# Delta rule and MLP on one core: bit masks by wide operations, norms' squares on another engine, a new written order

## The chip, the cores and the metric

The kernel runs on one core of one Trainium2 chip. The metric is the device time of one execution in microseconds, lower is better. A core has TensorE (PE in the profile; PEld is its weight load), VectorE (DVE), ScalarE (ACT), GpSimd (POOL) and SyncE (SP, which only issues DMAs here).

## The reference

```python
# q, k, v: (4, 8, 768, 48), beta: (4, 8, 768)
k_n = k / (np.linalg.norm(k, axis=-1, keepdims=True) + 1e-06)
for t in range(768):
    y[:, :, t] = q_t @ state
    v_old = state^T k_t
    state = state + beta_t * outer(k_t, v_t - v_old)
x = y as (4, 768, 384)              # 8 heads of 48 side by side
xn = (x - mean) / sqrt(var + 1e-06) * g_ln
out = x + relu(xn @ w_ch1) @ w_ch2  # 384 -> 1536 -> 384
```

All values are float32, but the two weight matrices arrive as 64-bit floats, which the kernel converts to float32 itself.

## The kernel before

The 768 tokens are cut into 12 chunks of 64 (`C`). Within a chunk the recurrence is a triangular system: with G the products of the chunk's keys, scaled by beta and the norms, the kernel needs the inverse of a unit triangular 64x64 matrix for each of 32 heads. These stand as 16 blocks on each half of the 128 partitions, in two halves `g` of 8.

Chunk 0 gets its inverse by doubling (`first_inverse`): from 1x1 blocks to 2x2 and so on to 64x64. Each of the steps n = 1 to 5 is a product E (`prod_e`, L720), a `copy_predicated` by mask n on DVE that keeps only the elements that this step adds (L727), a product Z (`prod_z`, L737), a transpose on DVE (`nat`, L685) and three copies on ACT (`back`, L679). It begins with mask 0 on the scaled products (L693, L702, L708). Both halves g go through it side by side. The chunks after it get their blocks of 32 rows on DVE, a column at a time (`rows_inverse`, L827 to L863, two instructions a column), while PE does other work, and the 32-blocks are joined on PE (`join`).

The masks: bit n of (row XOR column) has to be the highest that is set, and bit n of the row (for n = 0, of the column) must be set. The set-up writes `xor` and `bits` with two iotas on POOL, and makes each of the six masks with three DVE instructions on 128x64 integers (L395, L402, L408), in scratch that lies in `xb`, the tile in which `rows_inverse` works later: its memset (L827) has to wait for the masks. `eye`, the identity, is copied into six tiles (`BEGIN`), in which the doubling's steps accumulate (L421 on POOL, L426 on ACT).

`first_norms` makes for chunk 0 the norms of k: ACT squares (L594), DVE sums (L595), ACT takes the root (L596), DVE adds 1e-6 (L597), multiplies the result by itself (L598), takes the reciprocal (L599) and multiplies by beta (L602). A square root of `eps` (L439) runs early on ACT, so that the table of the root is loaded by then.

`recur` does a chunk: the u product (L996), y, the new state, the layer norm; `mlp(0)` runs as plain products in two halves, later chunks by schemes with fewer products (seven instead of eight, fifteen instead of eighteen). The weights come in pieces (`fetch`, on ACT's DMA queue) into `words` and `h_all` and are converted by two ACT instructions (L524, L532), one on DVE (L529) and an addition on POOL (L542).

Nothing is issued in program order. Each step is added to a list with what it reads and writes, and `ORDER`, a string of step numbers written out in the file, says in which order all are issued (`z` is a warm-up product on zeros). `in_this_order` then holds each engine's queue, and the queue of DMAs over SP and ACT, to this order. So each engine works strictly down its own list, and an instruction that waits holds up all behind it on that engine. The numbers `0.17`, `port=2` and so on beside a step are the planner's costs and do nothing at run time.

Of the kernel before, what the change touches and what calls it, by code (L numbers as in the profile page):

```python
# [9 lines left out]
I32 = mybir.dt.int32  # L10
# [6 lines left out]
C = 64  # L17
# [46 lines left out]
146 232 230 149 326 150 219 669 154 z 209 234 155 156 208 231 233 210 158 157 251 46 235 164 160 162 327 200 161 328 239 201 411 159 413 165 170 166  # L64
# [136 lines left out]
def kernel(  # L201
# [150 lines left out]
    def c_pool(fn, cost, w, r=(), pr=-200, **kw):  # L352
        add("Pool", cost, fn, r, w, pr=pr, **kw)
# [1295 lines left out]
```

## Time and profile before

| | |
|---|---|
| three timed runs | 507.06, 510.91, 511.09 us (median 510.91) |
| the profiled execution | 506.83 us, its span 505.1 us |
| PE | 485.9 us busy (96%), 9606 matmuls |
| PEld | 445.7 us busy (88%) |
| DVE | 355.2 us busy (70%), 774 instructions |
| POOL | 275.7 us busy (55%) |
| ACT | 249.0 us busy (49%) |
| DMA | 54.99 MB, of 196097 packets 186076 under 512 B |
| TensorE's granted clock, mean | 0.973; 0.5 from about 14.7 to 21.2, 25 to 32 and 42 to 55.7 us |

Busy time is the time in which an engine has an instruction in work, as a share of the span of 505.1 us. The span is the profiled execution from its first to its last instruction; the execution's own time is 1.7 us longer. The mean of an engine over the whole span hides that the first 50 us are limited otherwise than the rest, so the profile is read by stage.

### The profile page before, as it was taken

To read this page: it belongs to the slowest core of one execution; us is meant where nothing else is said; L and a number is where in the kernel's file an instruction comes from. 1 tells how busy PE (TensorE), PEld (TensorE's weight loads), DVE (VectorE), ACT (ScalarE), POOL (GpSimd) and SP (SyncE) were. 2 spreads that over 40 slices of the span, in tenths; PEclk is the share of its full clock that TensorE was granted. 3 is DMA by queue.
4 is the path that set the end of the run, shared out by engine and by line. 5 is a ranking of instruction groups with operands and counts; after the bars stand their busy time and mean duration, and the time that the engine had idled before them with its cause. 6 is when DMAs were issued, how large, how long until landed. Compare 5 with 4: busy or idle time off the path is not lost.

```text
span 505.1 us, 22184 instructions
## 1 busy us (share of the span) xinstructions
PE 485.9 (96%) x9606; PEld 445.7 (88%) x9606; DVE 355.2 (70%) x774; ACT 249.0 (49%) x620; POOL 275.7 (55%) x430
## 2 busy tenths in 40 slices
PE   6777999999999999999999999999999999999996
PEld 3666988688988898899999999999999999999996
DVE  9689987997699458886559898478899238143251
ACT  5777772633645434636444544436563347363230
POOL 5464527255754595629893462591642851645643
PEclk9776799999999999999999999999999999999999
DMA  8979896756646676448734434765245412111101
GB/s 173 308 153 187 270 189 79 107 138 133 90 87 106 192 127 114 46 100 205 155 41 64 102 55 153 150 91 87 57 85 136 82 23 58 43 50 46 31 12 31
DMA packets 196097, 54.99 MB, mean 109 GB/s; under 512 B 186076, under 2 KB 189404, under 8 KB 196000
## 3 DMA queue, kind: packets, MB, share of 16 engines
q1 hardware_dynamic: 189920, 40.58, 42.1%
q10 hardware_dynamic: 3872, 9.83, 6.1%
q0 software_dynamic: 2208, 3.17, 3.7%
q8 instruction: 75, 1.23, 1.0%
q14 instruction: 22, 0.18, 0.1%
HBM read 36.64 MB, written 16.91 MB: 106 GB/s over the span
## 4 chain that ended last, share of the span: by engine, by line
PE 78%; DVE 13%; SPq 3%; issue 2%; POOL 1%; DMA 1%; ACT 1%; ACTq 0%; DVEq 0%; POOLq 0%
PE f L1419 31%; PE f L1217 22%; PE f L1296 6%; DVE xb L863 4%; DVE tmp L856 4%; SPq L349 3%; PE by L1020 2%; PE two L1013 2%; PE by L979 2%; PE by L771 2%; PE two L979 2%; PE two L1030 1%; PE two L771 1%; PE by L894 1%; PE by L900 1%
## 5 line engine op out<-in xcount | busy, mean ns | idle before, releaser
L1406 POOL TENSOR_TENSOR h_all<-h_all 128x256 f32<-128x256 f32 x123 | 90.2, 746 | 133.3 <-PE f L1419 103.7
L1419 PE MATMUL f<-w_sb,h_all 128*128 128x192 f32 x492 | 109.5, 332 | 0.0
L1419 PE MATMUL f<-words,h_all 128*128 128x192 f32 x396 | 84.5, 330 | 0.3 <-POOL h_all L1406 0.3
L1419 PEld LDWEIGHTS f<-w_sb,h_all 128*128 128x128 f32 x492 | 81.8, 190 | 1.8 <-DVE o L1437 0.2
L863 DVE TENSOR_TENSOR xb<-xb,tmp 128x87 f32<-128x87 f32 (+21 forms) x186 | 73.7, 396 | 4.8
L856 DVE TENSOR_TENSOR tmp<-xb,gb 128x87 f32<-128x87 f32 (+21 forms) x186 | 73.1, 393 | 4.9
L1237 DVE TENSOR_TENSOR h_all<-h_all,f 128x512 f32<-128x512 f32 x96 | 63.6, 682 | 14.2 <-PE f L1217 13.1
L1419 PEld LDWEIGHTS f<-words,h_all 128*128 128x128 f32 x396 | 66.6, 190 | 1.7 <-POOL h_all L1406 1.0
L1296 PE MATMUL f<-xnt,w_sb 128*128 128x256 f32 x216 | 50.2, 382 | 0.0
L349 POOL DMA_DIRECT2D tb<-in_k_dram x64 | 41.9, 660 | 10.3 <-DVE kt L751 9.4
L1239 ACT ACTIVATE h_all<-h_all 128x512 f32<-128x512 f32 x48 | 28.5, 624 | 34.4 <-DVE h_all L1237 34.0
L1296 PEld LDWEIGHTS f<-xnt,w_sb 128*128 128x128 f32 x216 | 40.2, 190 | 5.2
L1233 ACT COPY h_all<-f 128x512 f32<-128x512 f32 x48 | 26.3, 590 | 33.9 <-PE f L1217 17.1
L1437 DVE TENSOR_TENSOR o<-f,x 128x192 f32<-128x192 f32 x33 | 11.6, 352 | 41.8 <-PE f L1419 25.9
L1217 PE MATMUL f<-words,w_sb 128*128 128x128 f32 x256 | 31.7, 276 | 0.0
L1305 ACT ACTIVATE h_all<-f 128x256 f32<-128x256 f32 x36 | 13.4, 383 | 34.8 <-PE f L1296 34.8
L1217 PEld LDWEIGHTS f<-words,w_sb 128*128 128x128 f32 x256 | 30.0, 192 | 0.2
L1217 PE MATMUL f<-xnt,w_sb 128*128 128x128 f32 x192 | 25.4, 276 | 0.0
L542 POOL TENSOR_TENSOR w_sb<-words 128x768 uint32<-128x768 uint32 (+1 forms) x11 | 15.0, 1364 | 17.7 <-DVE words L529 16.7
L1217 PEld LDWEIGHTS f<-xnt,w_sb 128*128 128x128 f32 x192 | 23.7, 192 | 0.1
L1322 PEld LDWEIGHTS f<-xnt,w_sb 128*128 128x128 f32 x144 | 19.5, 203 | 3.4 <-ACT h_all L1330 0.2
L1084 ACT ACTIVATE xnt<-xnt,g_sb 128x256 f32<-128x256 f32 x27 | 12.5, 499 | 19.2 <-DMA xnt<-xld 19.1
(246 smaller groups left out, 955.0 us busy)
## 6 DMA issues: line engine op xcount, KB each, us to landing
words<-in_moe_w_ch_dram ACTq DMA_DIRECT2D x10, 768.0 KB, 7.8
gd<-gsb SPq DMA_DIRECT2D x11, 512.0 KB, 3.9
v<-in_v_dram SPq DMA_DIRECT2D x24, 192.0 KB, 4.2
kr<-in_k_dram SPq DMA_DIRECT2D x46, 96.0 KB, 3.9
out_dram<-o SPq DMA_DIRECT2D x44, 96.0 KB, 2.4
xld<-xlt SPq DMA_DIRECT2D x9, 384.0 KB, 3.0
xnt<-xld SPq DMA_DIRECT2D x36, 96.0 KB, 3.3
gb<-gd SPq DMA_DIRECT2D x44, 64.0 KB, 3.0
```

Of the source, the lines that this page charges most:

```text
L349: add(eng, cost, lambda: QUEUE[eng].dma_start(out=out_, in_=in_), r, w, bulk=n * ns / 16e3, **kw)
L856: lambda j=j, n=n, w=w, t=t: nc.vector.tensor_tensor(out=t, in0=xv[:, 0:n, j : j + 1].to_broadcast([np_, n, w]), in1=gv[:, j : j + 1, j + ...
L863: "DVE", dve(n * w), lambda t=t, rest=rest: nc.vector.tensor_tensor(out=rest, in0=rest, in1=t, op=ALU.subtract),
L979: nc.tensor.matmul(dst[half(e), hp, j], src[drows(hp), (e if n else key_half(c, hp, e)) * GP + j], s_all[drows(hp), e, j], start=(n == 0 o ...
L1217: nc.tensor.matmul(wide(p[:, 128 * n : 128 * n + 128]), w[n // 2][:, n % 2 * 128 : n % 2 * 128 + 128], r, start=start and n == 0, stop=Tru ...
L1233: add("ACT", act(512), lambda: nc.scalar.copy(o, p), pk, ok)
L1237: add("DVE", dve(512), lambda: nc.vector.tensor_tensor(out=o, in0=o, in1=p, op=op), pk, ok)
L1239: add("ACT", act(512), lambda: nc.scalar.activation(o, o, ACTF.Relu), [], ok)
L1296: nc.tensor.matmul(p[:, 0:TOK], w1_sb[:, t, f * 128 : (f + 1) * 128], xnt[:, t], start=(t == 0), stop=(t == KC - 1))
L1322: nc.tensor.matmul(p[:, 0:128], w1_sb[:, t, f * 128 : (f + 1) * 128], xnt[:, t, cols], start=(t == 0), stop=(t == KC - 1))
L1406: add(eng, cost, lambda: e.tensor_tensor(out=out_, in0=x, in1=y, op=op), r, w, port=2 if eng == "Pool" else 1, pr=-2)
L1419: lambda f=f, t=start and f == 0: nc.tensor.matmul(p[:, 0:D2], lhs(f), rhs[:, f], start=t, stop=(f == F2 - 1), skip_group_check=True),
```

## The change

The six masks are made at once. POOL writes a third iota (`steps`, the numbers 0 to 5). `both` holds the row (or column) number shifted left by 16 and joined with `xor`; one shift of it by all values of `steps` (a 128x5x64 operation for masks 1 to 5, a 128x64 one for mask 0), one AND with 65536 + 63 and one comparison with 65537 give the masks: a field of the low bits that is 1 after the shift and a set bit 16. In `first_norms` the DVE product is replaced by a Square on ACT with `eps` as bias, on the root before 1e-6 is added. `ORDER` is written anew for all 2981 steps (2991 before); every other step does what it did.

```diff
     c_pool(lambda: nc.gpsimd.iota(bits, pattern=[[1, C]], base=0, channel_multiplier=0), 0.2, ["bits"])
+    flat = xb.rearrange("p s t -> p (s t)").bitcast(I32)
+    rows_, both, steps = flat[:, 960:1024], flat[:, 832:960].rearrange("p (n t) -> p n t", t=C), flat[:, 800:806]
+    wide = flat[:, 0 : 6 * C].rearrange("p (n t) -> p n t", t=C)
+    c_pool(lambda: nc.gpsimd.iota(steps, pattern=[[1, 6]], base=0, channel_multiplier=0), 0.15, ["steps"])
...
     MASKED = (0, 1, 2, 3, 4, 5)
-    for n in MASKED:
...
-            lambda t1=t1, k_=k_, w=w: nc.vector.tensor_scalar(
-                out=t1, in0=xor[:, 0:w], scalar1=w - 1, scalar2=k_, op0=ALU.bitwise_and, op1=ALU.logical_shift_right
...
-            lambda t2=t2, k_=k_, own=own: nc.vector.tensor_scalar(
-                out=t2, in0=own, scalar1=k_, scalar2=1, op0=ALU.logical_shift_right, op1=ALU.bitwise_and
...
-            lambda m=m, t1=t1, t2=t2: nc.vector.scalar_tensor_tensor(
-                out=m, in0=t1, scalar=1, in1=t2, op0=ALU.is_equal, op1=ALU.mult
...
+    for n, (own, key) in enumerate(((bits, "bits"), (rows_, "rows"))):
+            lambda n=n, own=own: nc.vector.scalar_tensor_tensor(
+                out=both[:, n], in0=own, scalar=16, in1=xor, op0=ALU.logical_shift_left, op1=ALU.bitwise_or
...
+    for n in range(2):
+        ns_ = slice(0, 1) if n == 0 else slice(1, 6)
...
+            lambda n=n, ns_=ns_, m_=m_: nc.vector.tensor_tensor(
+                out=wide[:, ns_], in0=both[:, n : n + 1].to_broadcast([128, m_, C]),
+                in1=steps[:, ns_, None].to_broadcast([128, m_, C]), op=ALU.logical_shift_right,
...
+            lambda ns_=ns_: nc.vector.tensor_scalar(
+                out=wide[:, ns_], in0=wide[:, ns_], scalar1=65536 + C - 1, scalar2=None, op0=ALU.bitwise_and
...
+            lambda ns_=ns_: nc.vector.tensor_scalar(
+                out=small[:, ns_].bitcast(I32), in0=wide[:, ns_], scalar1=65537, scalar2=None, op0=ALU.is_equal
...
             add("ACT", 0.21, lambda ss=ss, nr=nr: nc.scalar.sqrt(nr, ss), ks, kn_, **kw)
+            add("ACT", 0.21, lambda nr=nr, nd=nd: nc.scalar.activation(nd, nr, ACTF.Square, bias=eps), kn_ + ["eps"], kd, **kw)
             add("DVE", 0.17, lambda nr=nr: nc.vector.tensor_scalar_add(nr, nr, 1e-6), [], kn_, port=2, **kw)
-            add("DVE", 0.17, lambda nr=nr, nd=nd: nc.vector.tensor_tensor(out=nd, in0=nr, in1=nr, op=ALU.mult), kn_, kd, port=1, **kw)
             add("DVE", 0.2, lambda nd=nd: nc.vector.reciprocal(nd, nd), [], kd, port=2, **kw)
```

The new file is seven lines longer, so a line number of the changed kernel from L428 on is that of the kernel before plus 7 (L529 is L536 there).

At the head of the queues the new order is this. SP issues one of the four pieces of chunk 1's k before its two pieces of chunk 0's k. ACT issues the first 768 KB weight piece right behind its two pieces of chunk 0's k; then come two copies of `eye`, the root of `eps`, a third copy, and then the squares. POOL writes the three iotas and issues both beta rows, and copies `eye` twice before the second instruction of PE's identity `ident`; from the L834 memset of `xb` (which waits for masks 1 to 5) on, conversions, the scaling of v and DMA issues follow. DVE makes masks 1 to 5 up to the comparison, then `eye`, then mask 0; the comparison for masks 1 to 5 stands behind the first transposes of the doubling. From about 50 us on, PE's list is that of before with neighbouring steps exchanged.

More of the change, by code (lines that the diff above doesn't have):

```diff
@@ L59 @@
 ORDER = """
[4 rows of a table removed]
-146 232 230 149 326 150 219 669 154 z 209 234 155 156 208 231 233 210 158 157 251 46 235 164 160 162 327 200 161 328 239 201 411 159 413 165 170 166
[88 rows of a table removed]
+6 37 4 42 45 8 9 53 40 39 58 11 52 12 41 3 0 10 5 15 44 19 61 20 46 14 1 13 16 17 26 22 43 24 18 62 27 55 38 7 28 50 234 318 25 34 67 78 71 64 68 66
+63 72 69 79 23 65 85 73 70 51 74 80 86 81 75 217 76 54 77 83 87 60 82 100 88 z 89 84 106 90 101 59 194 91 207 102 103 92 107 205 112 105 108 195 110
[91 rows of a table added]
 """
@@ L375 @@
     c_pool(lambda: nc.gpsimd.iota(bits, pattern=[[1, C]], base=0, channel_multiplier=0), 0.2, ["bits"])
+    flat = xb.rearrange("p s t -> p (s t)").bitcast(I32)
+    rows_, both, steps = flat[:, 960:1024], flat[:, 832:960].rearrange("p (n t) -> p n t", t=C), flat[:, 800:806]
+    wide = flat[:, 0 : 6 * C].rearrange("p (n t) -> p n t", t=C)
+    c_pool(lambda: nc.gpsimd.iota(steps, pattern=[[1, 6]], base=0, channel_multiplier=0), 0.15, ["steps"])
     c_dve(
-        lambda: nc.vector.tensor_scalar(out=xor, in0=xor, scalar1=C - 1, scalar2=None, op0=ALU.bitwise_and),
-        0.17, ["xor"], port=2,
+        lambda: nc.vector.tensor_scalar(out=rows_, in0=xor, scalar1=C - 1, scalar2=None, op0=ALU.bitwise_and),
+        0.17, ["rows"], ["xor"], port=2,
     )
     c_dve(
-        lambda: nc.vector.tensor_tensor(out=xor, in0=xor, in1=bits, op=ALU.bitwise_xor), 0.22, ["xor"], ["bits"], port=1,
+        lambda: nc.vector.tensor_tensor(out=xor, in0=rows_, in1=bits, op=ALU.bitwise_xor), 0.22, ["xor"], ["rows", "bits"], port=1,
     )
-    flat = xb.rearrange("p s t -> p (s t)").bitcast(I32)
     c_dve(
@@ L386 @@
     )
-    c_dve(
-        lambda: nc.vector.tensor_tensor(out=flat[:, 960:1024], in0=xor, in1=bits, op=ALU.bitwise_xor), 0.22, ["rows"], ["xor", "bits"], port=1,
-    )
     MASKED = (0, 1, 2, 3, 4, 5)
-    for n in MASKED:
-        k_, m, w = n, masks[n], C
-        t1, t2 = (flat[:, C * i : C * i + w] for i in (2 * n, 2 * n + 1))
+    for n, (own, key) in enumerate(((bits, "bits"), (rows_, "rows"))):
         c_dve(
-            lambda t1=t1, k_=k_, w=w: nc.vector.tensor_scalar(
-                out=t1, in0=xor[:, 0:w], scalar1=w - 1, scalar2=k_, op0=ALU.bitwise_and, op1=ALU.logical_shift_right
+            lambda n=n, own=own: nc.vector.scalar_tensor_tensor(
+                out=both[:, n], in0=own, scalar=16, in1=xor, op0=ALU.logical_shift_left, op1=ALU.bitwise_or
@@ L397 @@
             ),
-            0.17, [("ma", n)], ["xor"], port=2,
+            0.22, [("both", n)], [key, "xor"], port=1,
         )
-        own = flat[:, 960 : 960 + w] if n else bits[:, 0:w]
+    for n in range(2):
+        ns_ = slice(0, 1) if n == 0 else slice(1, 6)
+        m_ = ns_.stop - ns_.start
         c_dve(
-            lambda t2=t2, k_=k_, own=own: nc.vector.tensor_scalar(
-                out=t2, in0=own, scalar1=k_, scalar2=1, op0=ALU.logical_shift_right, op1=ALU.bitwise_and
+            lambda n=n, ns_=ns_, m_=m_: nc.vector.tensor_tensor(
+                out=wide[:, ns_], in0=both[:, n : n + 1].to_broadcast([128, m_, C]),
+                in1=steps[:, ns_, None].to_broadcast([128, m_, C]), op=ALU.logical_shift_right,
@@ L404 @@
             ),
-            0.18, [("mb", n)], ["bits", "rows"], port=2,
+            0.08 + 0.07 * m_, [("ma", n)], [("both", n), "steps"], port=1,
         )
         c_dve(
-            lambda m=m, t1=t1, t2=t2: nc.vector.scalar_tensor_tensor(
-                out=m, in0=t1, scalar=1, in1=t2, op0=ALU.is_equal, op1=ALU.mult
+            lambda ns_=ns_: nc.vector.tensor_scalar(
+                out=wide[:, ns_], in0=wide[:, ns_], scalar1=65536 + C - 1, scalar2=None, op0=ALU.bitwise_and
             ),
-            0.22, [("mask", n)], [("ma", n), ("mb", n)], port=1,
+            0.1 + 0.04 * m_, [("ma", n)], [], port=2,
@@ L412 @@
         )
-    MASK_SCRATCH = [(x, n) for x in ("ma", "mb") for n in MASKED] + ["rows"]
+        c_dve(
+            lambda ns_=ns_: nc.vector.tensor_scalar(
+                out=small[:, ns_].bitcast(I32), in0=wide[:, ns_], scalar1=65537, scalar2=None, op0=ALU.is_equal
+            ),
+            0.1 + 0.04 * m_, [("mask", k) for k in range(ns_.start, ns_.stop)], [("ma", n)], port=2,
+        )
+    MASK_SCRATCH = [("ma", 0), ("ma", 1), ("both", 0), ("both", 1), "rows", "steps"]
     BEGIN = [(kts[2], "kt", 2), (gsbs[2], "g", 2), (gsbs[3], "g", 3), (xts[2], "xt", 2), (xts[3], "xt", 3), (pts[1], "pt", 1)]
```

183 rows, old and new, of the table ORDER are left out of this document.

## The prediction

> **What bounds the kernel now.** I read the page's head, the busy table by stage, TensorE's waits, and then the timeline of the first 26 us. By stage:
>
> ```profile
> core 0: us, PE busy (x) PEld busy (x) DVE busy (x) ACT busy (x) POOL busy (x), PEclk, DMA share, GB/s
> 0.00:6.00 6.00, 3.41 (x5) 1.24 (x6) 4.98 (x13) 1.55 (x3) 4.96 (x15) 1.00 0.60 103
> 6.00:12.00 6.00, 4.83 (x90) 3.20 (x90) 5.82 (x28) 4.63 (x12) 1.65 (x3) 1.00 1.13 242
> ...
> 40.00:50.00 10.00, 7.69 (x224) 6.87 (x228) 8.76 (x30) 7.85 (x20) 5.13 (x6) 0.60 0.93 166
> ...
> 100.00:300.00 200.00, 199.32 (x4277) 182.69 (x4276) 152.39 (x321) 93.30 (x244) 126.57 (x197) 1.00 0.58 111
> 300.00:490.00 190.00, 190.00 (x3286) 184.17 (x3285) 115.05 (x235) 90.77 (x211) 92.86 (x155) 1.00 0.34 73
> ```
>
> From 50 us to 490 us PE stands idle 0.7 us in all: there the order of PE's queue costs nothing and PE's own work (the same in both programs) sets the time. Before 50 us PE is idle for 14 us, and VectorE (DVE) is the fullest engine (5.82 of 6 us, 8.76 of 10): this is chunk 0's doubling inverse, a chain of matmuls E1, Z1 ... E5, Z5 with a masked copy and transposes on DVE between them. What shortens this chain brings PE's full stretch forward by as much, and the end with it. Why DVE is late there:
>
> ```profile
> 1.90 1.47 DVE L395 TENSOR_SCALAR xb<-u 128x64 int32<-128x64 int32 x1
> ...
> 2.26 1.28 ACT L439 ACT_TABLE_LOAD   x1 [2.26 <-issue]
> ...
> 3.80 2.38 DVE L402 TENSOR_SCALAR xb<-xb 128x64 int32<-128x64 int32 x1
> ...
> 5.93 0.52 ACT L594 ACTIVATE xln<-kr 128x384 f32<-128x384 f32 x1 [2.18 <-DMA kr<-in_k_dram]
> ...
> 8.10 0.54 DVE L595 TENSOR_REDUCE ksum<-xln 128x8 f32<-128x384 f32 x1
> ...
> 13.47 0.69 PE L720 MATMUL two<-qt,gsb 64*64 64x64 f32 x32 [0.19 <-DVE qt L708]
> ...
> 19.99 1.13 PE L737 MATMUL by<-xt,gsb 64*64 64x64 f32 x32
> ...
> 22.60 1.38 DVE L529 TENSOR_SCALAR words<-words 128x384 uint32<-128x384 uint32 x1
> ...
> 24.58 0.39 PE L771 MATMUL f<-qt,kt 48*64 48x64 f32 x10 [2.41 <-issue]
> ```
>
> Each row: start, length, engine, line, operation, and in brackets the idle time before it and what ended it. A mask step (L395, L402) takes 0.2 us alone (3.59 and 3.70 in the same timeline), but 1.47 and 2.38 us while GpSimd (POOL) runs memsets or copies; the L529 step, 0.33 us alone, took 1.38 us beside POOL's L542. The first half's squares (L594) end at 6.45 us, and their sum (L595) starts only at 8.10, behind masks. E1 starts at 13.47, the second half's Z1 at 19.99, and E2 behind it at 20.8. At 22.17 PE stops for 2.41 us for no cause that the profile shows.
>
> **The change, part by part.**
>
> *Masks.* DVE loses 22 narrow set-up steps and gets 11 (777 instructions become 764 with the two norm steps). Before, DVE was busy 4.98 and 5.82 us of the first two 6 us. The wide steps are not in the trace. The 128x320 shift lies between L863 at 64x240 (0.40) and L693 at 128x512 (0.68): 0.5, nearer the first. The 128x320 TENSOR_SCALAR steps lie between 0.33 (L529, 128x384, alone) and 1.38 (beside POOL): 0.35 each, because POOL stands waiting both times: first for `eye`, then, in its L834 memset of xb, for the wide mask itself. POOL's new iota stands behind two beta DMA issues (0.72 and 0.53), done at about 2.95; the wide shift waits for that. Shift, and, one 64-wide step and a memset follow, so `eye` comes at about 4.35 (3.40 before). ident's affine_select, now behind two POOL copies of `eye` (0.6 each), ends at about 5.9 (3.70 before). Chunk 0's k, landing at 5.93 before, covers that; without this cover each us that `eye` is late would be a us of PE's first transposes.
>
> *ScalarE (ACT).* Two norm products (0.16 each) leave DVE, two Squares (0.2, like L596's square root) join ACT. But the copies of `eye` now stand ahead of the square root that warms the table, and the built program holds two table loads for the one before: 1.28 us more. ACT: two k DMAs and the weight DMA to 2.6, load to 3.9, `eye` at 4.35, two copies (0.52 apart) to 5.4, load to 6.7, root and copy to 7.4. The squares start at 7.4 instead of 5.93. SP now issues a piece of chunk 1's k first (0.64 us), and the 768 KB weight DMA goes at 2.2 instead of 7.04 us, beside k: chunk 0's k lands at 6.5 to 7.2, inside ACT's delay.
>
> The Trainium skill ("ScalarE: Activation LUTs", What ACT_TABLE_LOAD costs) puts a switch of sets at 1.28 us and a drain of 1.38 us behind it. The trace shows 1.28 and the next activation 0.01 us later (2.26 + 1.28, then 3.55), so I add no drain; by the page the gain summed below would shrink by 1.38 us, to almost nothing.
>
> *To E2.* Squares to 8.3; two kt copies and the first root to 9.55 on ACT, the second kt copy to 10.1, the first Square at 10.25, the second at 10.65. On DVE 0.17 + 0.20 + 0.17 + 0.20 + 0.1 follow: the first gsb product starts at about 11.2 (11.15 before). Now both halves are multiplied first (0.65 + 0.1 + 0.63), then the masked copy (0.73) and transpose (0.72): E1 at 14.05, **0.6 later**. The second half: E1 at 14.05 + 1.45 = 15.5 (16.94 before). Wide mask 0.35, masked copies 0.73 + 0.27 + 0.73 to 17.55. Its Z1 then waits only for four q transposes, not eight: about 18.0 (19.99). E2 at about 18.65 against 20.8: **2.1 us earlier**.
>
> *E2 to the first u product (L996).* PE's 2.41 us stop lies 350 matmuls into its queue; I keep it at that count. Z2 then ends at 23.2 (25.74), E3 starts at 26.2 (29.3). Between E3 and E5 stand five weight steps L536 (0.33 to 1.38 each), and POOL, held until the wide mask, now works through copies, conversions and DMA issues without a pause from 16 to 32 us. beta_f's second DMA, at 22.20 before, goes at about 27.8 and took up to 6.1 to land: it holds DVE's db_b step until 33 or so, with a masked copy of E4 behind it. E5 comes at 37.6 with cheap steps and at 40.2 with dear ones (40.10 before), so 2.5 earlier to 0.1 later; the middle is 1.2 earlier. From E5 to the u product before: 45.92 - 40.10 = 5.8, of which 0.48 is a stop. After: DVE does four small steps, a weight step, a query product (0.62), a transpose and then the masked copy, 0.6 to 1.2 us later than before; the q/k transposes and Z5 that follow wait for less. I give 0.4 us of gain: **1.6 us earlier** in all. Bounds: 6.0 earlier (3.1 at E3 kept, 0.5 of the second stop, 2.4 of the first gone) and 5.6 later (below).
>
> *The rest.* Step by step PE's order after 50 us is the old one with neighbours exchanged (mean shift under 0.2 us of PE work in every stretch of 60 steps), and PE has the same 4839 instructions. The last 14 products of the tail come in nearly the same order. Cost: nothing, hidden by PE's full queue; without it each shift would count once.
>
> Sum: profiled execution 506.83 (span 505.1 and 1.7 around it) - 1.6 = 505.2. The four executions shown, 506.83, 507.06, 510.91 and 511.09, have the mean 508.97; the profiled one lies 2.1 below it and 4.1 below the median. TensorE's clock was 0.5 in three stretches between 14.7 and 55.7 us and full elsewhere; where these fall I can't forecast. I predict from the mean: 508.97 - 1.6 = **507.4**.
>
> **The rivals.**
>
> *A larger gain.* DVE sheds its masks, E and Z of both halves alternate without holes, and the 2.41 us stop vanishes as its traffic moves. 3.1 + 0.5 + 2.4 = 6.0: 503.0. For it: PE has 14 us of holes to give, the second half's Z1 waited for work that has moved. Against: the stop sits at a place in the queue that both have.
>
> *Slower: POOL and DVE collide.* Place: 16 to 38 us. POOL's queue stands behind the wide mask, then runs solid; each L536 on DVE waits for a POOL conversion. Seven of them (two of chunk words, five to E5) at 1.38 instead of 0.33 are 7.3 us; beta_f's late landing adds 1. Less the lead of 2.1 and 0.6 that it covers: 5.6 later, 514.6. It decides from a mean L536 of 0.7 us on, where the lead is gone. For it: the 2.38 and 1.38 rows. Against: L529 at 31.15 and 35.88 took 0.34 each with POOL at work, so not every one is caught.
>
> *The lead is eaten.* E2 comes earlier, but the weight steps or the k DMAs take all of it before the first u product: 509.0. For it: two table loads and the dearer E5 stage. Against: 2.1 us at E2 by rows.
>
> **How the numbers follow.** Forecast 0.45 (range 504 to 509.5 alone), larger gain 0.30, eaten 0.12, slower 0.13. A difference of 1% (5.1 us) is about what a measurement here can tell. The first and third cases are within it (0.57), the second beyond it (0.30), the fourth beyond it (0.13). The range takes in the gain's 503.0 less half the runs' spread (2.1) and stops short of most of the slower case: 501.0 to 513.5.
>
> **What would show it.** Right: two table loads on ACT, squares at about 7.4, E1 near 14, E2 near 18.7, the u product near 44, then PE full with the same 455 us of work. Wrong: E2 later than 20.8 (the head's delays counted too low), L536 above 0.7 on average, PE holes after 50 us (the new order is not neutral), or no stop on PE near matmul 350 (then the larger gain).

## The result, and the profile after

The changed kernel takes 511.10 us (median of 21 runs, 509.03 to 513.81), the kernel before 509.38 us (21 runs, 506.47 to 511.89). The ratio is 1.0046 (95% interval 1.0028 to 1.0064): 2.3 us slower, where 1.6 us faster was forecast; within 1%, but on the other side. The profiled execution of after has a span of 508.5 us, that of before 505.1; the one of before was a quick one (506.83 against a median of 509.38), so the 3.4 us between the two profiles are more than the runs show. The mean granted clock is 0.977 (0.973 before) and explains none of it.

By stage (busy time and number of instructions of PE, PEld, DVE, ACT, POOL, then the granted clock, the DMA share and GB/s), kernel after:

```profile
core 0: us, PE busy (x) PEld busy (x) DVE busy (x) ACT busy (x) POOL busy (x), PEclk, DMA share, GB/s
...
6.00:12.00 6.00, 2.42 (x17) 1.78 (x17) 0.62 (x3) 2.34 (x5) 1.24 (x3) 1.00 1.28 196
...
50.00:60.00 10.00, 7.74 (x199) 6.91 (x191) 8.87 (x18) 5.77 (x18) 5.37 (x5) 0.58 0.81 232
...
100.00:300.00 200.00, 199.80 (x4209) 181.59 (x4207) 150.48 (x322) 93.27 (x249) 123.64 (x191) 1.00 0.59 114
300.00:490.00 190.00, 190.00 (x3405) 183.94 (x3405) 116.17 (x240) 89.10 (x211) 92.65 (x155) 1.00 0.35 74
```

From 60 us on PE is idle for 0.5 us in all up to 490 us (0.7 before): it is full, as before. The loss lies in two stretches. From 6 to 12 us PE is busy 2.42 us (4.83 before) and DVE 0.62 (5.82 before): everybody waits, while the DMA engines are full. From 50 to 60 us a second hole has opened. The timeline of after says why:

```profile
2.26 0.65 ACTq L349 DMA_DIRECT2D words<-in_moe_w_ch_dram  x1
...
2.92 0.49 DVE L402 TENSOR_TENSOR xb<-xb 128x320 int32<-128x320 int32 x1 [0.37 <-POOL xb L379]
2.94 1.28 ACT L433 ACT_TABLE_LOAD   x1 [2.94 <-issue]
...
4.10 0.13 DVE L388 TENSOR_SCALAR u<-u 128x64 f32<-128x64 int32 x1
...
5.41 1.28 ACT L446 ACT_TABLE_LOAD   x1
...
9.87 0.94 ACT L601 ACTIVATE xln<-kr 128x384 f32<-128x384 f32 x2 [2.45 <-DMA kr<-in_k_dram]
9.89 1.09 PE L575 MATMUL by<-ident,kr 128*128 128x128 f32 x4 [3.58 <-DMA kr<-in_k_dram]
...
12.39 0.58 ACT L580 COPY kt<-by 128x512 f32<-128x512 f32 x1 [1.59 <-PE by L575]
...
17.90 0.69 PE L727 MATMUL two<-qt,gsb 64*64 64x64 f32 x32
...
22.53 0.69 PE L727 MATMUL two<-qt,gsb 64*64 64x64 f32 x32
...
39.16 0.18 DVE L847 TENSOR_TENSOR db_b<-db_b,beta_f 64x32 f32<-64x32 f32 x1 [0.58 <-DMA beta_f<-in_beta_dram]
...
52.80 1.90 DVE L956 TENSOR_SCALAR xln<-x,mv 128x384 f32<-128x384 f32 x1
...
52.99 1.48 POOL L549 TENSOR_TENSOR w_sb<-words 128x768 uint32<-128x768 uint32 x1
...
54.75 0.90 PE L1099 MATMUL two<-ident,xln 128*128 128x128 f32 x3 [2.26 <-DVE xln L956]
```

The kernel before, at the places that match:

```profile
20.89 0.94 PE L720 MATMUL two<-qt,gsb 64*64 64x64 f32 x32
...
45.92 0.98 PE L996 MATMUL two<-v,xt 64*64 64x48 f32 x25 [0.48 <-issue]
...
49.95 0.40 DVE L949 TENSOR_SCALAR xln<-x,mv 128x384 f32<-128x384 f32 x1
...
51.18 0.90 PE L1092 MATMUL two<-ident,xln 128*128 128x128 f32 x3
```

Chunk 0's k lands at 9.87 us (5.93 before). E1 starts at 17.90 (13.47 before), E2 at 22.53 (20.89 before). At 52.80 the layer norm's step, 0.40 us before, takes 1.90 beside POOL's addition, and PE waits 2.26 us for it.

### The profile page after: what moved, and what is told of

The parts are those of the page before. It is cut to its first block, busy times and chain, and to the rows that moved or that the text cites. A ratio compares the mean times of both kernels' runs of the same rounds, so it can differ in the third digit from the quotient of the medians.

```text
span 508.5 us, 22143 instructions
## 1 busy us (share of the span) xinstructions
PE 486.5 (96%) x9606; PEld 444.8 (87%) x9606; DVE 349.0 (69%) x761; ACT 248.0 (49%) x623; POOL 276.7 (54%) x431
## 3 DMA queue, kind: packets, MB, share of 16 engines
q8 instruction: 75, 1.23, 1.0%
## 4 chain that ended last, share of the span: by engine, by line
PE 89%; DMA 3%; ACT 2%; POOL 1%; DVE 1%; issue 1%; SPq 1%; ACTq 0%; DVEq 0%; POOLq 0%
PE f L1426 31%; PE f L1224 22%; PE f L1303 10%; PE f L1329 3%; PE f L1344 3%; PE by L1027 2%; PE by L986 2%; PE two L986 2%; PE two L1020 2%; PE by L778 2%; PE two L778 2%; PE two L1037 2%; DMA kr<-in_k_dram 1%; DMA beta_f<-in_beta_dram 1%; PE by L901 1%
## 5 line engine op out<-in xcount | busy, mean ns | idle before, releaser
L1426 PE MATMUL f<-w_sb,h_all 128*128 128x192 f32 x492 | 108.2, 331 | 0.0
L1303 PE MATMUL f<-xnt,w_sb 128*128 128x256 f32 x216 | 51.8, 385 | 0.1
L1303 PEld LDWEIGHTS f<-xnt,w_sb 128*128 128x128 f32 x216 | 39.8, 190 | 6.5 <-ACT xnt L1114 0.8
L1224 PE MATMUL f<-words,w_sb 128*128 128x128 f32 x256 | 33.1, 278 | 0.0
L1065 ACT ACTIVATE x<-by 128x384 f32<-128x384 f32 x23 | 11.1, 489 | 26.8 <-PE by L1027 18.4
L1224 PEld LDWEIGHTS f<-xnt,w_sb 128*128 128x128 f32 x192 | 23.6, 192 | 0.1
L629 POOL TENSOR_TENSOR v<-v,knrm 128x768 f32<-128x768 f32 x11 | 16.7, 1520 | 12.3 <-DMA v<-in_v_dram 11.9
```

What stands on the lines that cost most here:

```text
L1224: nc.tensor.matmul(wide(p[:, 128 * n : 128 * n + 128]), w[n // 2][:, n % 2 * 128 : n % 2 * 128 + 128], r, start=start and n == 0, stop=Tru ...
L1303: nc.tensor.matmul(p[:, 0:TOK], w1_sb[:, t, f * 128 : (f + 1) * 128], xnt[:, t], start=(t == 0), stop=(t == KC - 1))
L1426: lambda f=f, t=start and f == 0: nc.tensor.matmul(p[:, 0:D2], lhs(f), rhs[:, f], start=t, stop=(f == F2 - 1), skip_group_check=True),
```

## The experiments

Most are the changed kernel with steps moved in `ORDER`; e6 is the kernel before with one step moved, and m1, m2, m2b and h2 mix the two. Ratios are to the kernel before on the same chip, with the 95% interval (0.001 is 0.5 us); they, not the medians, are compared between runs of different chips. The changed kernel's is 1.0046. Two runs whose ratios lie less than about 1.3 us apart are not resolved by their intervals.

### What makes k late

```diff
 ACT: k of chunk 0 (2 pieces)
-     first weight piece, 768 KB          (e1, e3)
 ...  squares, first kt copy
+     first weight piece, 768 KB          (e1, e3)
-SP:  one piece of chunk 1's k            (e2, e3)
 SP:  k of chunk 0 (2 pieces)
+     one piece of chunk 1's k            (e2, e3)
```

> The changed kernel with one step moved: the first 768 KB weight transfer is issued on ScalarE behind the first kt copy, where the kernel before has it, and no longer at 2.26 us right behind chunk 0's k. Theory W (the weight transfer shares the DMA engines with the small packets of k and holds them up): chunk 0's k lands at 6.0 to 7.0 us instead of 9.87; the squares then wait for ScalarE's second table load and start at about 7.4; E1 of the first half at about 15.4 instead of 17.9, E2 about 20.3 instead of 22.5; the time 1.5 to 2.5 us below the changed kernel's. Theory S (the piece of chunk 1's k that SP issues ahead of chunk 0's pieces is what delays them): k still lands after 9.2 us, E1 after 17.2, the time within 0.5 us of the changed kernel's.

> The changed kernel with one step moved: SP issues its two pieces of chunk 0's k first, and the piece of chunk 1's k behind them. Theory S: k lands at 6.0 to 7.0 us, squares at about 7.4, E1 at about 15.4, the time 1.5 to 2.5 us below the changed kernel's. Theory W: k lands only the 0.6 us of one issue earlier (9.2 to 9.9), E1 at 17.2 to 17.9, the time within 0.7 us of the changed kernel's.

> The changed kernel with both moves: the weight transfer behind the first kt copy, and chunk 0's k first on SP. Both theories: k lands at 5.9 to 6.5 us as before. Then the second table load on ScalarE (5.41 to 6.69) is what the squares wait for: they start at about 7.4, 1.5 us later than in the kernel before; E1 15.0 to 15.6, E2 19.6 to 20.4. If a loss at the start passes through to the end, the time is 2.0 to 2.8 us below the changed kernel's, so about level with the kernel before (within 0.6 us). If the later losses (beta_f's transfer, the layer norm's step that stood 1.9 us beside GpSimd) are losses of their own and not of the late k, less than 1 us comes back.

The transplant, in the kernel before:

```diff
 ACT: k of chunk 0 (2 pieces)
+     first weight piece, 768 KB
 ...  first kt copy
-     first weight piece, 768 KB
```

> The kernel before with one step moved: the first 768 KB weight transfer is issued on ScalarE right behind its two pieces of chunk 0's k, as the changed kernel does, and everything else stays. Theory W: chunk 0's k lands at 8.5 to 10 us instead of 5.93, E1 at 16 to 17.5 instead of 13.47, and the time is 2 to 3.5 us above the kernel before, as far as nothing behind it absorbs the delay. Theory S: k lands at 5.9 to 6.5 us, E1 at 13.5 to 14.1, the time within 0.6 us of the kernel before.

Timeline of the run with the weights later, and then of the kernel before with the weights early:

```profile
6.46 0.63 PE L575 MATMUL by<-ident,kr 128*128 128x128 f32 x4 [0.15 <-DMA kr<-in_k_dram]
...
7.33 0.93 ACT L601 ACTIVATE xln<-kr 128x384 f32<-128x384 f32 x2
...
7.94 0.37 ACTq L349 DMA_DIRECT2D words<-in_moe_w_ch_dram  x1
```

```profile
2.25 0.64 ACTq L349 DMA_DIRECT2D words<-in_moe_w_ch_dram  x1
...
9.54 0.52 ACT L594 ACTIVATE xln<-kr 128x384 f32<-128x384 f32 x1 [5.12 <-DMA kr<-in_k_dram]
```

Theory W holds both ways: taking the weight transfer away brings k from 9.87 to 6.46, adding it to the kernel before takes k from 5.93 to 9.54, and there it costs 2.7 us (512.23 us, ratio 1.0054, 1.0026 to 1.0081). The order on SP alone moves k to 9.37 only (e2: 511.87 us, 1.0048, 1.0028 to 1.0069). The Trainium skill ("DMA: Bandwidth & Descriptors", Queues, rings and completion order) says that each DMA engine takes turns between the queues it has work for, a packet at a time; these landings agree with that, since k's pieces on SP's queue land later when weights are issued on ACT's; the turns themselves no run here shows.

But the end hardly came back: e1 511.04 us (1.0034, 1.0011 to 1.0056), e3 510.37 us (1.0023, 1.0000 to 1.0046), against an expected 1.5 to 2.8 us less than the changed kernel; 0.6 and 1.1 us less were measured, neither resolved. E1 came at 15.7 in e1 and only at 16.4 in e3. The timeline of e3 shows the next obstacle on ACT:

```profile
13.98 0.55 ACT L531 ACTIVATE words<-words 128x384 f32<-128x384 f32 x1 [3.52 <-DMA words<-in_moe_w_ch_dram]
...
14.43 1.05 ACT L580 COPY kt<-f 128x512 f32<-128x512 f32 x2
```

The new order put the first weight conversion ahead of chunk 1's kt copies, which suits early weights. With later weights it waits 3.52 us for them, and the copies and E1 behind it.

### The conversions behind the copies

```diff
 ACT: (as e3)
-     three conversions of the first weight piece
      kt copies of chunk 1, first xt copies
+     three conversions of the first weight piece
```

> The run with both moves at the start (weight transfer behind the first kt copy, chunk 0's k first on SP), and besides ScalarE's three conversions of the first weight piece put behind the first copies of chunk 1's kt and of xt, as the kernel before has them; in that run the first conversion waited 3.52 us for the weights, and the kt copies and E1 behind it. Theory Q (the queue of ScalarE was what kept the early k from paying): the kt copies of chunk 1 at about 11.5 us, E1 at 13.6 to 14.0 instead of 16.4, E2 at 18.3 to 19.0; if that holds to the end, 2.5 to 3 us less than that run, so 1.5 to 2.5 us below the kernel before. Rival P (further on the order has places that are tied to other work, the weight steps on VectorE at 27 to 30 us and E3 of the second half at 32.1 us in both runs): E2 early as said, but E3 of the second half still after 31.5 us, and the time within 0.8 us of that run.

Measured 509.37 us (1.0015, 0.9995 to 1.0036), 1.6 us below the changed kernel. E1 started at 13.66 as theory Q said; E2 only at 20.51, and E3 of the second half at 30.55, between the two theories. The time, 0.4 us below e3, is what rival P said. Its timeline, PE and DVE:

```profile
17.30 0.37 PE L727 MATMUL by<-qt,gsb 64*64 64x64 f32 x2 [1.58 <-issue]
...
26.22 0.52 DVE L536 TENSOR_SCALAR words<-words 128x768 uint32<-128x768 uint32 x1
27.72 0.56 DVE L536 TENSOR_SCALAR words<-words 128x768 uint32<-128x768 uint32 x1 [0.98 <-ACT words L531]
...
27.97 0.45 PE L727 MATMUL two<-qt,gsb 64*64 64x64 f32 x13 [1.05 <-issue]
...
28.20 0.44 DVE L692 STREAM_TRANSPOSE qt<-by 128x256 f32<-128x256 f32 x1
...
30.55 1.13 PE L727 MATMUL by<-qt,gsb 64*64 64x64 f32 x32 [2.13 <-ACT xt L686]
...
40.69 0.58 PE L744 MATMUL by<-xt,xt 64*64 64x64 f32 x11 [2.19 <-issue]
```

Two things hold it: two weight steps on DVE (one waits for ACT) ahead of the transposes of the second half, and stops of PE for which the profile names no releaser ("issue").

### The layer norm's step

```diff
 DVE: column step, column step
+     layer norm of chunk 0 (L956)
      weight step (L536)
      column step (L863)
-     layer norm of chunk 0 (L956)
```

> The changed kernel with one step moved: the layer norm's step of chunk 0 (L956) stands on VectorE ahead of a weight step (L536 at 52.04 us) and a column step (L863 at 52.51), so that it runs at about 52.1 us while GpSimd issues DMAs, and not at 52.8 beside GpSimd's L549 (52.7 to 54.2). Theory C (the collision is a loss of its own, on the path to TensorE's full stretch): L956 takes 0.4 to 0.6 us instead of 1.90, TensorE's wait ahead of L1099 falls from 2.26 us to 0.2 to 0.7, and the time falls by 1.5 to 2.0 us. Rival (that wait is slack of the order, and TensorE then waits as long for the next steps): the wait moves to L1003 or L1329, the time stays within 0.5 us of the changed kernel's.

```profile
51.71 2.13 POOL L349 DMA_DIRECT2D tb<-in_k_dram  x2
...
52.70 0.41 DVE L956 TENSOR_SCALAR xln<-x,mv 128x384 f32<-128x384 f32 x1
...
53.39 0.90 PE L1099 MATMUL two<-ident,xln 128*128 128x128 f32 x3
...
53.85 1.48 POOL L549 TENSOR_TENSOR w_sb<-words 128x768 uint32<-128x768 uint32 x1
```

Theory C holds: beside POOL's DMA issues the step takes 0.41 us, PE's 2.26 us wait is gone, and the time is 509.65 us (1.0019, 1.0006 to 1.0032), 1.4 us below the changed kernel. The move does two things: the step is 1.5 us shorter, and two steps of 0.9 us together no longer stand ahead of it; the run doesn't part them. The Trainium skill ("SBUF — State Buffer", Who interferes with whom) says that some VectorE operations, `tensor_scalar` among them, can use a port pair that they share with GpSimd, and that the loser waits for the other's whole instruction. 1.90 us beside a 1.48 us addition and 0.41 away from it agree with that; which of the two was issued first the rows leave open (VectorE's begins 0.19 us ahead).

### Both, and the rest mended

```diff
 g3 = f2 + layer norm's step first
 g1 = g3, and
 DVE: second half's two transposes
+     two weight steps (L536)             (were ahead of the transposes)
 ACT: three xt copies of the second half
+     three conversions                   (were ahead of the copies)
 POOL: beta_f's second half ahead of an addition
 g4 = g1, and on ACT the root of eps ahead of the copies of eye
```

> The run with the early k and the late conversions, and besides the layer norm's step of chunk 0 moved ahead as in the run that tested it alone. Theory of separate losses (the late k costs some 1.5 us of the end, the collision of the layer norm's step another 1.4): the two add up, 2.5 to 3.5 us below the changed kernel, a ratio to the kernel before of 0.997 to 1.000; TensorE's wait ahead of L1099 (2.70 us in the run with the early k) at most 0.7. Rival (one gain covers the other, since TensorE's stops fill what is freed): the ratio stays at 1.001 to 1.003.

> As the run before it, and in the E2 to E3 stage VectorE does the second half's two transposes ahead of two weight steps (L536), ScalarE the three xt copies that follow from them ahead of its conversions, and beta_f's second half is issued on GpSimd ahead of an addition. Theory D (the weight steps in the inverse's chain cost the order its gain): E3 of the second half at 28.0 to 29.3 us instead of 30.55, the wait for ScalarE's xt copy there under 0.8 us instead of 2.13, and the time 1 to 2 us below that of the run before it, a ratio to the kernel before of 0.994 to 0.997. Rival F (TensorE's instructions come in blocks of about 127 products over the same DMA engines, and its stops at products 475 and 730 hold the end): E3 of the second half earlier as said, but the stop at product 730 grows by as much, product 730 starts at 40 to 41.5 us as in all runs so far, and the time stays within 0.6 us of the run before it.

> As the run with the transposes first, and the root of eps stands ahead of ScalarE's first copy of the identity, so that one table load is left. Theory T (the second load is what the squares wait for once k is early): squares at 6.3 to 6.5 us instead of 7.32, E1 at 12.7 to 13.2 instead of 13.66. If that reaches the end, 0.5 to 1.0 us less. Rival F: TensorE's stop at product 221 (1.58 us at 15.7 us in the run with the early k) grows by 0.5 to 1.0 us and takes it; E2 and the time within 0.4 us of the run with the transposes first.

g3: 508.00 us (0.9971, 0.9954 to 0.9987). The two losses add up: 1.6 and 1.4 us alone, 3.8 together, no less than their sum. g1: 507.40 us (0.9960, 0.9941 to 0.9979), faster than both kernels, 4.4 us below the changed one; what it adds to g3 is not resolved. g4: 507.32 us (0.9967, 0.9947 to 0.9986). The squares start at 6.39, but E1 at 13.99, no earlier than in g1 (13.66), since the step behind them, ACT's kt copy, waits 1.15 us for PE's transposes and starts at 8.47 (8.16 in g1). No gain from the second table load is resolved at the end. Timeline of g1:

```profile
13.66 0.69 PE L727 MATMUL two<-qt,gsb 64*64 64x64 f32 x32 [0.19 <-DVE qt L715]
...
51.18 0.90 PE L1099 MATMUL two<-ident,xln 128*128 128x128 f32 x3
```

Neither theory of g1's expectation got its numbers: E3 of the second half came at 29.47 (28.0 to 29.3 expected), its wait for the xt copy was 0.96 us (under 0.8 expected); and the stop at product 730 was not there, against rival F.

### TensorE's stops

Counting PE's matmul records from the start, the stops called "issue" fall at the same counts in nearly every run, where they occur (a few records can be missing): 220 or 221 (0.29 us in the kernel before, 0.61 after, 1.58 in f2, 1.66 in g4), 347 or 348 (2.41 before, 1.60 in g1), 475 (0.70 after, 2.83 in g4), 730 (0.45 after, 2.19 in f2): 127 apart or a multiple of that. Their length varies from execution to execution: f1 has the lists of after up to 52 us, and yet stands 2.29 us at product 475.

```profile
30.90 0.45 PE L727 MATMUL two<-qt,gsb 64*64 64x64 f32 x13 [2.29 <-issue]
```

So two single profiles can differ by as much behind such a place without any cause in the order (1.6 us here, of which 0.66 was left at the u product). Next, the queue of instructions on the page of after; the same queue in g1 from 14.0 to 15.5 us, ahead of its stop at product 221; and the queue of the weights during that stop, from 15.7 to 16.8 us (packets, MB, share of the engines' time):

```profile
q8 instruction: 75, 1.23, 1.0%
```

```profile
q8 instruction: 1, 0.02, 5.8%
```

```profile
q10 hardware_dynamic: 83, 0.42, 97.4%
```

75 packets and 1.23 MB are 16.4 KB a packet. The Trainium skill ("Runtime: NRT & Kernel Launch", Instruction fetch mechanics) says that instructions come in blocks of 16 KiB, 256 instructions each, and that the crossing is mostly hidden. The blocks agree (127 products and as many weight loads; 9606 of each make 75 blocks of 256). Hidden the crossings are not in the first 65 us here.

The kept traces hold each packet of this queue, and they show what the stops are. In g1 a packet ended at 15.41 us and PE went on at 16.87; in after one ended at 27.72 and PE went on, at product 475, at 29.17; in f1 the same packet ended at 29.46, and PE went on at 30.90. In all runs, at every gap of over 0.5 us at one of these counts, up to 1238, PE goes on 1.1 to 1.9 us after the end of such a packet, and no block begins earlier than that. Where there is no stop, the packet had ended in time (g1 at 475: packet 26.14, product 27.87). So TensorE waits for its instructions there. The packet for a block begins 0.5 to 5.9 us after PE has entered the block ahead of it; what decides between early and late is open, and one run moved the weight transfers to see whether they do.

```diff
 g1, ACT:
-     second and third weight piece (10.16, 11.63 us), fourth (14.7 us)
 ...  first conversion
+     second and third weight piece
 ...  gsb copies
+     fourth weight piece
```

> The run with the transposes first, and the second and third weight pieces are issued on ScalarE behind the first conversion (about 15.2 us) instead of at 10.16 and 11.63 us, the fourth at about 18 instead of 14.7 us. Theory F (TensorE's next block of instructions comes over the same DMA engines and stands behind the weight packets: these held the engines 97% of the time in the stop at product 221): the stop at product 221 falls from 1.16 us to under 0.5, E1 of the second half is done 0.7 to 1.5 us earlier, E2 at 18.0 to 18.8 instead of 19.31; the later conversions may take it back further on, so the time within 1 us of the run with the transposes first. Rival (the stop has nothing to do with the weight transfers): it stays at 1.0 to 1.8 us.

The stop at 221 fell from 1.16 to 0.65 us, but not under 0.5, and stops of 1.74 us (475) and 1.63 us (984) came instead; E2 at 20.05 was not earlier, and the time is 508.94 us (0.9996, 0.9977 to 1.0015). The fall proves little: the packet ended at 15.25 us, only 0.16 earlier than in g1, PE came there 0.2 later, and h2 (below), which issues the second and third weight piece at 8.64 and 11.06 us, stood 0.70 us. That the weight transfers hold the instructions back is not shown.

### What the masks and norms are worth

m1 is the new masks in the old order, m2 the new masks and Squares in the old order; m2b is m2 with the write of `eps` first. h2 is the reverse: g1's order with the old masks and norms.

```diff
 m1, m2 (DVE, old order): xor, eye,
-     18 narrow mask steps among other work, eps
+     mask 0, eps, masks 1 to 5
 m2b: +eps ahead of all
```

> The kernel before with the new masks alone: its own norms and its own order, in which the eleven new mask steps stand where the old ones began (mask 0 first, all six by about 6 us). If the masks by themselves shorten the start: the sums of the norms (L602) start at about 6.5 instead of 8.10 us, E1 at 12.3 to 13.0 instead of 13.47, and the time is 0.5 to 1.5 us below the kernel before. If the start is bound elsewhere (ScalarE's copies, TensorE's stop of 2.4 us): E1 within 0.3 us of 13.47 and the time within 0.5 us of the kernel before.

> The kernel before with the new masks and with the squares of the norms on ScalarE, in its own order (each Square right behind its root): the whole change without the new order. One table load, as before. Theory M (masks and norms help by some tenths, the new order is what costs): E1 at 12.2 to 13.0 us, the time 0.5 to 1.7 us below the kernel before, that is 3 to 4 us below the changed kernel. Rival (masks and norms cost something of their own): the time level with the changed kernel.

> The kernel before with the new masks and the Squares on ScalarE in its own order, now with the write of eps first on VectorE (in the two runs of this kind so far it stood behind mask 0 and ran at 7.1 us, and the root of eps and the squares on ScalarE waited for it). Theory M (masks and norms help by themselves): squares at 5.9 to 6.1 us, E1 at 12.3 to 13.2 instead of 13.47, the time 0.5 to 1.5 us below the kernel before. Rival (the early time goes into stops of TensorE at products 220 and 347, where it stood 0.29 and 2.41 us before): E1 earlier as said, but product 347 starts at 24.0 to 25.0 us as before and the time within 0.5 us of the kernel before.

m1: 509.98 us (1.0031, 1.0007 to 1.0056), m2: 509.70 us (1.0028, 0.9999 to 1.0058). Both tell little: I had put `eps` behind mask 0, it was written at 7.10 us, and ACT's squares waited for its root until 7.34. m2b mends that (squares at 6.14) and is level with the kernel before: 509.70 us (0.9996, 0.9972 to 1.0020), but E1 was at 15.3 and not at 12.3 to 13.2. Its timeline:

```profile
3.82 2.36 DVE L408 TENSOR_SCALAR xb<-xb 128x64 int32<-128x64 int32 x1
6.21 0.94 DVE L414 TENSOR_SCALAR u<-xb 128x64 int32<-128x64 int32 x1
...
8.89 1.01 DVE L601 TENSOR_REDUCE ksum<-xln 128x8 f32<-128x384 f32 x2
...
10.93 1.08 DVE L604 TENSOR_SCALAR knrm<-knrm 128x8 f32<-128x8 f32 x2 [0.89 <-ACT ndb L603]
```

In the old order these steps run beside POOL's copies of `eye` (4.19 to 5.91 us) and are held for as long as the old ones were; the sums of the norms start at 8.89, not at 6.5. And since the masks were done earlier, POOL's next copies and memset (9.93 to 11.97 us) came earlier too and fell on the norms' two small steps L604 (1.0 us each instead of 0.17). Fewer steps do not help where the length of a step is set by POOL. E1 was 1.8 us later than in the kernel before, but PE's transpose of the layer norm came at 51.18 us in both profiles: this lateness was gone by then.

> The run with the transposes first, with the old masks (18 narrow steps and one for the rows) and the old norms (the product on VectorE) put back in the places of the new ones: the mended order alone. Theory N (VectorE has slack at the start, 1.5 us ahead of the beta copy and 1.1 ahead of the sums, and the masks as such are worth next to nothing): the old masks end at 6.5 to 7.3 us, the sums start at 8.3 as with the new ones, E1 at 13.5 to 13.9, the time within 0.6 us of the run with the transposes first, and below the kernel before. Rival M (the masks and norms carry the gain): sums at 9.3 or later, E1 at 14.5 or later, the time 1 us or more above the run with the transposes first.

```profile
7.38 0.23 DVE L408 SCALAR_TENSOR_TENSOR u<-xb 128x64 int32<-128x64 int32 x1
...
7.60 1.00 DVE L595 TENSOR_REDUCE ksum<-xln 128x8 f32<-128x384 f32 x2
...
14.31 0.69 PE L720 MATMUL two<-qt,gsb 64*64 64x64 f32 x32 [1.41 <-DVE qt L708]
```

h2: 507.40 us (0.9983, 0.9964 to 1.0002). The old masks end at 7.6 us, just as the squares are done, and E1 is 0.65 us later than in g1. Its interval and g1's (0.9941 to 0.9979) overlap: the ratios are 1.2 us apart, and by the two intervals anything from -0.2 to 2.5 us is possible, so whether masks and norms are worth something at the end stays open.

## Why the prediction was wrong

Profile against profile, by the prediction's own steps:

- **The step that failed: "chunk 0's k lands at 6.5 to 7.2 ..., inside ACT's delay."** It landed at 9.87. I had seen the weight DMA at 2.2 us "beside k" and given it and SP's new order together no more than 1.3 us; the weight DMA alone cost 3.4 (e1) to 3.6 (e6). So the squares came at 9.87 and not at 7.4, and E1 at 17.90 and not at 14.05. Of these 3.85 us, 2.47 are the squares; the other 1.4 come from work I had counted as done while ACT was late: PE's transposes of k ran beside the squares, and ACT's kt copy waited 1.59 us for them.
- **From E1 to E2: right in number, partly by luck.** 4.6 us forecast, 4.63 measured (7.42 before). The wide shift took 0.49 (0.5 forecast), the steps on 128x320 0.33 and 0.28 (0.35), `eye` was there at 4.23 (4.35). E2 was late by what E1 was late. But in f2, g3, g1 and g4, where k is early as I had assumed, this stretch takes 5.7 to 7.0 us, with a stop of 1.16 to 1.73 us at product 221 for which I had no term; E2 comes at 19.3 to 20.8, so of the 2.1 us forecast at E2 three of these four have under 0.4, and g1 has 1.6: most of it would not have come even with k on time.
- **Table loads: right,** two of 1.28 us; the next activation began 0.01 us after the second (6.70), so the drain that the Trainium skill ("ScalarE: Activation LUTs", What ACT_TABLE_LOAD costs) states is not in this trace either. In g4, without the second load, no gain at the end is resolved.
- **E2 to the u product:** the u product was forecast 1.6 us ahead of 45.92, so 25.7 us behind E2; it came at 46.78, 24.25 behind. So 1.4 us of the lateness were made good there (0.45 less, if one goes by the end of the product: of the 32 products before, 7 had run ahead of the stop at 45.92), though beta_f's second DMA was issued at 32.71 (27.8 forecast) and held DVE's L847 by 0.58 us and, behind it, E4's masked copy and a product of PE (1.32 us).
- **The stop "at a place in the queue that both have": half right.** The places are fixed counts, but every 127 products, and the length depends on when PE gets there and when the block's packet ends: 2.41 us at 347 before; 0.61, 0.70 and 0.45 at three others after.
- **Missing from the sum: the layer norm's step.** From the u product to PE's transpose of the layer norm 5.26 us before, 7.97 after: 2.7 lost (2.26 of them PE's wait, 0.45 the mark at 45.92 as above), for which I had no term and wrote "Cost: nothing", since I took "the old one with neighbours exchanged" on PE's list for all of it. DVE's list against POOL's was what mattered. f1 shows 1.4 us of it in timed runs.
- **"What shortens this chain brings PE's full stretch forward by as much": not borne out.** m2b was 1.8 us late at E1 and level at 51.18; e1 gained 2.2 us at E1 over the changed kernel and 0.6, not resolved, at the end.

Two of the signs that I had named for being wrong came: E2 later than 20.8 (the row before says 20.89), and a hole on PE after 50 us.

Sum: -1.6 + 3.85 - 1.4 + 2.7 = +3.55, against 3.4 between the two spans. In timed runs the late k and the collision are worth 3.8 us together (g3 against after), and without them the new order with its masks is 1.5 us faster than the kernel before, near the 1.6 forecast. That agreement is partly luck: E2 in g3 is at 20.75, not at the forecast 18.65.

Of the rivals, the slower one had the right kind of mechanism (DVE and POOL collide) at the wrong place: the weight steps L536 took 0.32 to 0.65 us after, not 1.38; steps outside its stretch were hit, L956 the one that PE waited for. "The lead is eaten" came nearest in size (509.0 against 511.10), but there was no lead at E2. The 2.41 us stop of the larger gain did vanish.

## What to carry to other kernels

Here a large transfer, issued beside small ones on another queue, delayed their landing by 3.4 to 3.6 us; where the small one opens the critical chain, hold the large one until it has landed, and then move what waits for the large one too. An order is a set of queues that fit each other: one early transfer mended alone gave back 0.6 us (not resolved), with the conversions that relied on it and one step at the far end 3.8. A VectorE step that stands directly ahead of a full TensorE belongs where GpSimd issues DMAs or is idle, not beside its additions.

## What was not expected of the hardware

In the first 65 us TensorE stops at fixed counts of its own instructions, 127 products apart, for 0.3 to 3.2 us (3.21 at product 475 in e6), and goes on 1.1 to 1.9 us after a packet of instructions ends. What is gained ahead of such a place can be lost in it: in g4 the stops at 221, 475 and 603 sum to 5.7 us, in the kernel after those seen up to 60 us to 1.8.
